# Block transposes from the tenth couple of heads on, with their loads, squares and sums moved

## The chip, the cores and the metric

The kernel runs on one core of a Trainium2 chip. Its engines work side by side, each through its own queue in order: TensorE (PE in the profile; its weight loads are PEld), VectorE (DVE), ScalarE (ACT), GpSimd (POOL) and SyncE (SP), which here issues nearly all DMAs. The metric is the device time of one execution in microseconds (us). All data is float32.

## The reference, cut to what matters

```python
q, k, v: (8, 12, 448, 64)      # batch, heads, sequence, head size
w_in: (768, 2048); w_out: (2048, 768)

def rmsnorm(x, g):
    return x / np.sqrt(np.mean(x * x, axis=-1, keepdims=True) + 1e-06) * g
scores = np.matmul(rmsnorm(q, g_q), rmsnorm(k, g_k).transpose(0, 1, 3, 2)) / np.sqrt(64)
attn = softmax(scores)                     # max subtracted, 1e-9 added to the sum
x = np.matmul(attn, v)                     # then (B,H,S,D) -> (B*S, H*D) = (3584, 768)
h = x @ w_in
out = (h * (1.0 / (1.0 + np.exp(-h)))) @ w_out
```

## The kernel before, in words

**Couples.** The 96 heads are handled in 24 couples of four heads (two pairs), three couples for each of the eight batches, six for each group of two batches (`GROUP` is 6). For couple c, `visit(c)` does the attention: 56 score matmuls (L726, each pair of records one matmul), exponentials on ScalarE (L731) that take k's norm as their scale, and 56 records of the weighted sum with v (L763). The softmax sums are made of the exponentials by adds on VectorE (`add`, L777) and a product with ones on TensorE (`sum_up`, L799). VectorE inverts them (L808), DMAs spread the factors over the partitions (L815, L817), and the next visit multiplies with them (L824).

**Hand-over.** After visit c comes `between(c)`, which prepares couple c+1 and fills TensorE with work of the feed-forward layer: products with `w_in` (L923) in the seven-product form of Strassen (class `Seven`), for the group of batches finished before. `fill` runs such matmuls up to a due amount, and deals other work between them: `others` evenly, one after so many steps, `prompt` one at the start and one after each product. There are two fills for a couple, called the first and the second half here. A step is one 448-column product of 128 rows (two records), three steps make a product. Products alternate between two PSUM banks (tile mm; `bank`); with `turns["third"]` and more than five steps due, every other product goes to a buffer of the scores' tile (sc) instead. A product is evicted by VectorE (L873) or by ScalarE (L931, L941), two additions of the seven go to GpSimd (L943, L944), and the finished rows get SiLU (L1061) and are stored to a scratch tensor `hidden` (L956).

**Two ways to transposed q and k.** q and k must lie with the head dimension on the partitions. Up to couple 11 TensorE transposes them: q with 8 matmuls (`transpose_q`, L643), k with 7 (`transpose_k`, L661). ScalarE copies both out of PSUM (L647, and L663, which multiplies with the gains). q's norm comes from squares on ScalarE (L470) and reductions on VectorE (L471), two for each half of q, then a power and a product on GpSimd (L499, L514). From couple `LATE` = 12 on q and k are loaded in quarters, so that VectorE's transpose of 32x32 blocks is enough (`load_quarters`, L253: eight DMAs of 128-byte runs; `flip`, L669 for q, L672 for k, then the gains on ScalarE, L678). q's squares are then taken in one operation (L686) and reduced in one (L687); TensorE adds the two halves of each head (`scale`, L698, with the identity changed once by `pair_up`), and GpSimd does power and product (L702, L705). k is loaded a second time by rows, for its norm (L285, L287, squares L470, L471). From couple 8 on q has only one place, q0; the places k0 and k1 serve couples in turn, and from `LATE` on k0 holds the rows and k1 the quarters.

**Other work in couples 6 to 11.** The last parts of `w_in` are loaded and rounded there: `weights_in` deals steps named r (`round`: three operations on VectorE, L124, L127, L131, then one on GpSimd, L135, then a load, L86) and o (`open`: two on ScalarE, L101 and L102) into the halves. Visits 8 and 10 hold two rounds each, and visits 7 and 9 four sums of weights each (`sum_w_in`, L870, L873). The remaining four sums stand in `sums_halves`: three in the first half of couple 10, one in its second.

**What sets the order.** It is written out by hand: the program order of each engine is the order of the calls. A queue that waits holds back all that was issued on it later. Couple numbers begin at 0, so couple 9 is the tenth.

Of the kernel before, what the change touches and what calls it, by code (L numbers as in the profile page):

```python
# [30 lines left out]
class Shapes:  # L31
    def __init__(self, q, w_in):
        self.B, self.H, self.S, self.D = q.shape
        self.DM, self.DFF = w_in.shape
        self.P = 128
        self.J = 4
        self.R = self.S // self.J
        self.NPAIR = self.H // 2
        self.NW = self.DM // self.P
        self.NF = self.DFF // self.P  # L40
        self.HALF = self.DM // 2
        self.FULL = self.S // self.P
        self.REST = self.S - self.FULL * self.P

        self.KEYS = self.S // self.P
        self.LEFT = self.S - self.KEYS * self.P
        assert 2 * self.LEFT == self.P and self.NPAIR % 2 == 0 and self.LEFT == self.D

        self.KA, self.KL, self.KB = 0, 2 * self.KEYS * self.D, 2 * (self.KEYS + 1) * self.D
        self.NK = self.KB + 2 * self.KEYS * self.D  # L50
        assert 2 * self.D == self.P and self.J * self.R == self.S and 2 * self.REST == self.P
        assert self.NW == self.NPAIR and self.B % 2 == 0

        self.LATE = 2 * self.NPAIR
        self.Q = 32
        assert 2 * self.S == self.NK and 4 * self.Q == self.P and self.D == 2 * self.Q

# [136 lines left out]
def kernel(  # L194
# [77 lines left out]

    def load_k_quarters(c):
        b, cp = divmod(c, z.NPAIR // 2)
        load_quarters(k[b, ts(cp, 4)], place["k1"])

    def load_k(c):
        t = place[f"k{c % 2}"]
        if c >= z.LATE:
            t = place["k0"]  # L280
            for i, start in enumerate((z.KA, z.KB)):
                main, left = plain(k, c, i)
                dst = t[:, ds(start, z.KL)].rearrange("p (j h d) -> p h j d", j=z.KEYS, h=2)
                for h in range(2):
                    nc.sync.dma_start(dst[:, h], main[:, h])  # L285
                dst = t[ds(i * z.LEFT, z.LEFT), ds(z.KL, 2 * D)]
                nc.sync.dma_start(dst.rearrange("p (h d) -> p h d", h=2), left)  # L287
            return
        main, left = keys_of(k, c)
        for i, start in enumerate((z.KA, z.KB)):  # L290
            dst = t[:, ds(start, z.KL)].rearrange("p (j h d) -> p j h d", j=z.KEYS, h=2)
            nc.sync.dma_start(dst, main[:, ts(i, 2)].rearrange("p h j d -> p j h d"))
            if i == 0:
                for m in range(2):
                    dst = t[ds(m * z.LEFT, z.LEFT), ds(z.KL, 2 * D)]
                    nc.sync.dma_start(dst.rearrange("p (h d) -> p h d", h=2), left[m])
# [242 lines left out]
def bounded(  # L539
# [12 lines left out]
    )  # L552
    GROUP, LATE = z.NPAIR, z.LATE
    EARLY = GROUP - 1


    hidden = dram.tile([z.NF, P, z.B * S], F32, name="hidden")
# [42 lines left out]
    def q_of(c):  # L600
        return rows_q[c % 2 if c < GROUP + 2 else 0]

    def load_q(c):

        if 0 < c < NC:
            loads["q"](c, raw_of(c) if c < GROUP else q_of(c))
# [59 lines left out]
    def flip(c, name):  # L666

        if name == "q":
            nc.vector.transpose(qT.rearrange("p i s -> p (i s)"), q_of(c)[:, 0 : z.NK])  # L669
            load_q(c + 1)  # L670
            return
        nc.vector.transpose(kT, place["k1"])  # L672
        if c + 1 < NC:
            loads["quarters"](c + 1)

# [3 lines left out]

    n = z.NK // z.Q  # L680

    def sum_squares(c):

        if c >= NC:
            return
        nc.scalar.activation(squares, q_of(c)[:, 0 : z.NK], AF.Square)  # L686
        nc.vector.tensor_reduce(  # L687
            out=norm.rms[c % 2][:, 0:n], in_=squares.rearrange("p (n e) -> p n e", e=z.Q),
            axis=AX.X, op=ALU.add,
        )  # L690
# [90 lines left out]
    def sum_up(c):  # L781

        n = D // 2
        early = c < GROUP
        t = bank(S) if c < GROUP else ps.tile([P, 2, BANK], F32, name="sc", bufs=2)[:, 0, 0:S]
        terms = [(0, lambda: weights(c, 0))]
        if early:  # L790
            terms = [(0, lambda: weights(c, LEFT - 1))] + terms + [(1, None)]
        if c == GROUP - 1:
            terms.insert(1, (0, lambda: weights(c, 1)))
        for k, (which, w) in enumerate(terms):
            if k == len(terms) - 2:
                yield
            for h in range(2):
                for i in range(2):
                    nc.tensor.matmul(  # L799
                        t[ds(h * D + i * n, n), :],  # L800
                        ones[:, which + i if which else 0],
                        left_weights(c)[:, h] if which else w()[:, i, h],
                        start=(k == 0), stop=(k == len(terms) - 1),
                    )

        def invert(half):
            rows = ts(half, S // 2)
            nc.vector.reciprocal(out=factors(c)[0][:, rows], in_=t[:, rows])  # L808

        def spread():  # L810
            mine = [a.rearrange("(h i p) s -> i h p s", h=2, i=2) for a in factors(c)]
            queues = (nc.sync, nc.gpsimd if c == GROUP - 1 else nc.sync)
            for h in range(2):
                for i in range(2):
                    queues[h].dma_start(mine[1][i, h], mine[0][1, h])  # L815
            for h in range(2):
                queues[h].dma_start(mine[0][1, h], mine[0][0, h])  # L817

        yield [lambda: invert(0), lambda: (invert(1), spread())]
# [8 lines left out]
    def normalise(c):  # L828


        def piece(name, i):
            t = scratch[i if c < GROUP + 2 else 0]
            source = raw_of(c) if c < GROUP else q_of(c)
            if name == "q":
                norm.squares_q(c, source, t, i)
            else:
                norm.squares_k(c, place["k0" if c >= LATE else f"k{c % 2}"], t, i)
            if name == "q" and c < GROUP:
                norm.root(c, name, i)
                norm.scale(c, source, q_of(c), i, nc.gpsimd)  # L840
                if i == 1 and c + 2 < GROUP:
                    load_q(c + 2)
            elif i == 1:
                norm.root(c, name)
                if name == "q":
                    for m in range(2):
                        norm.scale(c, source, q_of(c), m, nc.gpsimd)
                elif LATE <= c < NC - 1:
                    loads["k"](c + 1)

        if c >= NC:
            return []
        return [lambda a=a: piece(*a) for a in (("q", 0), ("q", 1), ("k", 0), ("k", 1))]
# [419 lines left out]
    def save_out(q, i, j):  # L1273
        for t in range(2):
            store(
                nc, out, z, (4 * q + 2 * (i - 1) + t) * P, results[i, j][t], (j - 1) * z.HALF,
                nc.gpsimd if q == QUADS - 1 and i == 2 else nc.sync, plain=4,
            )

    def quad(q):  # L1280
# [53 lines left out]
        if q == QUADS - 1:  # L1334

            def then(t, h):
                store(
                    nc, out, z, (4 * q + t) * P, c[1, 2][t][:, ts(h, QUARTER)],
                    z.HALF + h * QUARTER, *((nc.scalar, nc.sync)[:: 1 if h else -1]), plain=4,
                )  # L1340

            deep(3, c[1, 2], True, None, then)
            return
# [51 lines left out]
    for c in range(GROUP // 2):  # L1395
        halves[2 * (c - GROUP)], halves[2 * (c - GROUP) + 1] = "rr", "o"
    sums_halves = {-6: [(0, 0)], -4: [(0, 1)], -3: [(0, 2)], -2: [(0, 3)]}
    sums_halves[8] = [(3, step) for step in range(3)]
    sums_halves[9] = [(3, 3)]
    sums_visits = {GROUP + 1: 1, GROUP + 3: 2}  # L1400

    def weights_in(c, half):
# [90 lines left out]
    def between(c):  # L1493
# [30 lines left out]
        if c >= GROUP and c % GROUP == 0:  # L1524
# [2 lines left out]
            work = halves_in(last_two(c), range(HF), plain_in, dict(begun), fetched)  # L1527
            begin(work, columns, 2 * GROUP)
            begun.clear()
        late = add(c, LEFT - 1) + add(c, LEFT) if c >= GROUP else []  # L1530
        further = normalise(c + 2) if c >= GROUP - 1 else []
        fill(late + weights_in(c, 0) + (further[2:] if c >= GROUP else further[:2]))
        prompt = transposes_and_sums() if GROUP // 2 <= c != GROUP - 1 else []
        if prompt and c < GROUP:
            prompt.insert(0, lambda: None)
# [2 lines left out]
        if c >= LATE - 2:  # L1538
            if c == LATE - 2:
                prompt.append(pair_up)  # L1540
            queries = prompt[3:] + [lambda: sum_squares(c + 2)]
            steps = weights_in(c, 1)
            fill(steps + [lambda: None] * len(steps), prompt[:3] + [lambda: run_all(queries)])
        else:
            fill(weights_in(c, 1) + (further[:2] if c >= GROUP else []), prompt)
# [258 lines left out]
```

## Time and profile before

| | |
|---|---|
| runs | 1311.65, 1312.07, 1312.16 us; median 1312.07 |
| profiled execution | 1311.68 us, span 1309.9 us |
| mean granted TensorE clock | 0.999 |
| TensorE's transposes, q (L643, records of tile rows) | 60 records, 7.5 us busy |
| TensorE's transposes, k (L661) | 84 records, 11.6 us busy |
| ScalarE's copies out of PSUM (L647, L663) | 11 of 906 ns and 12 of 1002 ns |
| factors' product on TensorE (L698) | 24 records, 3.6 us busy |
| sums on TensorE in tile sc (L799) | 144 records, 18.5 us busy |

The span runs from the first to the last instruction, and the execution's time has a little more around it. Busy times of an engine that are hidden beside TensorE's cost nothing. A matmul's record ends after the next has begun, so TensorE's work is read from the distance between the starts of its records.

### The profile page before, as it was taken

To read this page: it belongs to the slowest core of one execution; us is meant where nothing else is said; L and a number is where in the kernel's file an instruction comes from. 1 tells how busy PE (TensorE), PEld (TensorE's weight loads), DVE (VectorE), ACT (ScalarE), POOL (GpSimd) and SP (SyncE) were. 2 spreads that over 40 slices of the span, in tenths; PEclk is the share of its full clock that TensorE was granted. 3 is DMA by queue.
4 is the path that set the end of the run, shared out by engine and by line. 5 is a ranking of instruction groups with operands and counts; after the bars stand their busy time and mean duration, and the time that the engine had idled before them with its cause. 6 is when DMAs were issued, how large, how long until landed. Compare 5 with 4: busy or idle time off the path is not lost.

```text
span 1309.9 us, 19866 instructions
## 1 busy us (share of the span) xinstructions
PE 1294.2 (99%) x7209; PEld 832.3 (64%) x7209; DVE 950.1 (73%) x1627; ACT 505.0 (39%) x886; POOL 360.8 (28%) x230
## 2 busy tenths in 40 slices
PE   9999999999999999999999999999999999999998
PEld 4444444444444444444444455558999999999998
DVE  6998777777655556755554786698978787878785
ACT  7866656645544545545544354310000000100000
POOL 6766544453334333334320244300000000000000
PEclk9999999999999999999999999999999999999999
DMA  9674335344443444444321457312323223231411
GB/s 242 169 198 121 100 98 164 113 95 110 108 94 90 121 96 95 98 113 95 83 68 63 141 191 253 125 61 78 106 81 101 85 95 110 68 127 52 136 42 40
DMA packets 249439, 144.94 MB, mean 111 GB/s; under 512 B 184292, under 2 KB 233220, under 8 KB 249332
## 3 DMA queue, kind: packets, MB, share of 16 engines
q1 hardware_dynamic: 248672, 142.42, 38.8%
q8 instruction: 59, 0.97, 0.3%
q0 software_dynamic: 352, 0.96, 0.2%
q14 instruction: 48, 0.39, 0.1%
q10 hardware_dynamic: 308, 0.20, 0.1%
HBM read 93.98 MB, written 41.29 MB: 103 GB/s over the span
## 4 chain that ended last, share of the span: by engine, by line
PE 94%; DVE 2%; ACT 2%; issue 1%; POOL 0%; ACTq 0%; DVEq 0%; POOLq 0%
PE alone L1230 23%; PE mm L923 22%; PE av L763 9%; PE sc L726 9%; PE sc L923 9%; PE mm L1230 8%; PE alone L923 7%; PE alone L1267 2%; PE sc L799 1%; PE mm L799 1%; PE mm L1267 1%; PE sc L643 1%; PE sc L661 1%; ACT work L731 1%; DVE work L777 0%
## 5 line engine op out<-in xcount | busy, mean ns | idle before, releaser
L731 ACT ACTIVATE work<-sc,rms 128x448 f32<-128x448 f32 x318 | 181.1, 634 | 63.1 <-PE sc L726 50.4
L923 PE MATMUL mm<-x,W 128*128 128x448 f32 x414 | 169.9, 545 | 4.0 <-DVE parts L873 1.8
L726 PE MATMUL sc<-work 64*64 64x448 f32 x1344 | 164.1, 544 | 1.8 <-ACT work L731 1.5
L777 DVE TENSOR_TENSOR work<-work 128x896 f32<-128x896 f32 (+1 forms) x114 | 124.6, 1125 | 50.0 <-PE av L763 49.5
L923 PE MATMUL mm<-sums_x,W 128*128 128x448 f32 x372 | 152.5, 543 | 0.5 <-DVE parts L873 0.5
L763 PE MATMUL av<-work,rows 64*64 64x448 f32 x1272 | 150.7, 540 | 0.5 <-DVE av L739 0.3
L499 POOL TENSOR_TENSOR rms<-rms,minus_half 128x14 f32<-128x14 f32 (+4 forms) x43 | 105.4, 2453 | 148.2 <-DVE rms L495 138.6
L923 PEld LDWEIGHTS mm<-x,W 128*128 128x128 f32 x414 | 76.4, 190 | 87.2 <-issue 73.7
L526 POOL DMA_DIRECT2D out_dram<-x x2 | 1.2, 592 | 443.3 <-DVE x L873 443.3
L923 PEld LDWEIGHTS mm<-sums_x,W 128*128 128x128 f32 x372 | 69.2, 190 | 73.7 <-issue 68.0
L1230 PE MATMUL alone<-W,rows 128*128 128x192 f32 x610 | 113.0, 326 | 0.0
L763 PEld LDWEIGHTS av<-work,rows 64*64 64x64 f32 x1272 | 57.8, 132 | 69.1 <-issue 33.8
L1230 PEld LDWEIGHTS alone<-W,rows 128*128 128x128 f32 x610 | 101.5, 190 | 0.0
L726 PEld LDWEIGHTS sc<-work 64*64 64x64 f32 x1344 | 52.9, 132 | 74.1 <-ACT work L731 30.8
L943 POOL TENSOR_TENSOR parts<-parts,stage 128x448 f32<-128x448 f32 x31 | 41.9, 1351 | 146.7 <-DVE parts L873 146.3
L923 PE MATMUL sc<-x,W 128*128 128x448 f32 x198 | 80.6, 543 | 0.0
L702 POOL TENSOR_TENSOR rms<-rms,minus_half 128x28 f32<-128x28 f32 x12 | 57.5, 4792 | 61.7 <-DVE rms L699 61.7
L1230 PE MATMUL alone<-W,work 128*128 128x192 f32 x382 | 72.2, 326 | 0.0
L1061 ACT ACTIVATE stage<-stage 128x896 f32<-128x896 f32 x63 | 57.3, 945 | 21.9 <-DVE stage L873 21.0
L1240 ACT COPY rows<-alone 128x192 f32<-128x192 f32 x33 | 10.5, 318 | 141.6 <-PE alone L1230 78.2
L1230 PEld LDWEIGHTS alone<-W,work 128*128 128x128 f32 x382 | 63.8, 190 | 0.0
L923 PEld LDWEIGHTS sc<-x,W 128*128 128x128 f32 x198 | 36.9, 190 | 39.6 <-issue 37.2
(259 smaller groups left out, 2283.6 us busy)
## 6 DMA issues: line engine op xcount, KB each, us to landing
hidden<-stage SPq DMA_DIRECT2D x63, 448.0 KB, 3.2
work<-hidden SPq DMA_DIRECT2D x21, 1024.0 KB, 5.1
rows<-in_moe_w_out_dram SPq DMA_DIRECT2D x32, 384.0 KB, 3.3
W<-in_moe_w_in_dram SPq DMA_DIRECT2D x22, 512.0 KB, 5.2
x<-hidden SPq DMA_DIRECT2D x7, 1024.0 KB, 6.4
work<-work SPq DMA_DIRECT2D x111, 56.0 KB, 2.0
rows<-in_q_dram SPq DMA_DIRECT2D x96, 56.0 KB, 2.2
rows<-in_k_dram SPq DMA_DIRECT2D x96, 56.0 KB, 2.2
```

What stands on the lines that cost most here:

```text
L499: nc.gpsimd.tensor_tensor(out=t, in0=t, in1=half, op=ALU.pow)
L702: nc.gpsimd.tensor_tensor(out=f, in0=f, in1=minus_half.to_broadcast([P, n]), op=ALU.pow)
L726: nc.tensor.matmul(two[ds(half * D, D), h, 0:S], keys[rows, ts(half, D)], qT[rows, pair, :], start=True, stop=True,)
L731: nc.scalar.activation(left_weights(c)[:, h] if j == LEFT else weights(c, j)[:, i, h], two[:, h, 0:S], AF.Exp, scale=norm.column(c, i, h, j),)
L763: nc.tensor.matmul(sums[i][ds(h * D, D), :], v, w, start=(j == 0 and step == 1), stop=(j == LEFT - 1 and step == 1),)
L777: nc.vector.tensor_tensor(out=total, in0=total, in1=more, op=ALU.add)
L799: nc.tensor.matmul(t[ds(h * D + i * n, n), :], ones[:, which + i if which else 0], left_weights(c)[:, h] if which else w()[:, i, h], start ...
L923: nc.tensor.matmul(t, self.left(name, s), self.right(name, s), start=s == ends[0], stop=s == ends[1])
L943: nc.gpsimd.tensor_tensor(out=u2, in0=u2, in1=p5, op=ALU.add)
L1061: nc.scalar.activation(t, t, AF.Silu)
L1230: nc.tensor.matmul(t, x[:, i], y, start=i == ORDER[0], stop=i == ORDER[-1])
L1267: nc.tensor.matmul(o, a[:, 2 * i + m, t], right_one(name, i)[:, m], start=n == 0, stop=n == len(steps) - 1,)
```

## The change

Couples 9, 10 and 11 are loaded in quarters too and transposed in blocks by VectorE. As couple 9 is odd, k0 and k1 change roles for the late couples. The result's rows are stored in plain order from batch 3 on.

For the hand-overs from couple 8 to couple 10, q's load for the couple after next is no longer issued in `flip` at the start of the half but in the middle of the first half's `others`. For the hand-overs from 7 to 10 the squares of q are dealt together with the third prompt piece (pair_up in 7, k's flip after), one product before their reduction. The third bank is closed for the second half in all hand-overs before 11. In couple 10 the left-over sums aren't added on VectorE any more: `sum_up` takes four matmuls more, straight from the left-over weights. Of the last four sums of weights two stand in each half of couple 10.

```diff
-        self.LATE = 2 * self.NPAIR
+        self.LATE = 3 * self.NPAIR // 2
+        self.PLAIN = 3
+        self.BY_ROWS, self.BY_QUARTERS = f"k{self.LATE % 2}", f"k{1 - self.LATE % 2}"
...
     def load_k_quarters(c):
         b, cp = divmod(c, z.NPAIR // 2)
-        load_quarters(k[b, ts(cp, 4)], place["k1"])
+        load_quarters(k[b, ts(cp, 4)], place[z.BY_QUARTERS])
...
         if c >= z.LATE:
-            t = place["k0"]
+            t = place[z.BY_ROWS]
...
+    SOON = 2 * GROUP - 1
+    FULL = SOON - 1
...
             nc.vector.transpose(qT.rearrange("p i s -> p (i s)"), q_of(c)[:, 0 : z.NK])
-            load_q(c + 1)
+            if c > SOON:
+                load_q(c + 1)
             return
-        nc.vector.transpose(kT, place["k1"])
+        nc.vector.transpose(kT, place[z.BY_QUARTERS])
...
+    def square(c):
+
+        if c < NC:
+            nc.scalar.activation(squares, q_of(c)[:, 0 : z.NK], AF.Square)
+
     def sum_squares(c):
 
         if c >= NC:
             return
-        nc.scalar.activation(squares, q_of(c)[:, 0 : z.NK], AF.Square)
...
         if early:
             terms = [(0, lambda: weights(c, LEFT - 1))] + terms + [(1, None)]
+        if c == FULL:
+            terms.insert(0, (1, None))
...
-            if k == len(terms) - 2:
+            if early and k == len(terms) - 2:
                 yield
...
-    sums_halves[8] = [(3, step) for step in range(3)]
-    sums_halves[9] = [(3, 3)]
+    sums_halves[8] = [(3, 0), (3, 1)]
+    sums_halves[9] = [(3, 2), (3, 3)]
...
-        late = add(c, LEFT - 1) + add(c, LEFT) if c >= GROUP else []
+        late = add(c, LEFT - 1) if c >= GROUP else []
+        if c >= GROUP and c != FULL:
+            late += add(c, LEFT)
         further = normalise(c + 2) if c >= GROUP - 1 else []
-        fill(late + weights_in(c, 0) + (further[2:] if c >= GROUP else further[:2]))
+        late += weights_in(c, 0) + (further[2:] if c >= GROUP else further[:2])
+        if LATE - 1 <= c < SOON:
+            late.insert(len(late) // 2, lambda: load_q(c + 2))
+        fill(late)
+        if c < SOON:
+            turns["third"] = False
...
             queries = prompt[3:] + [lambda: sum_squares(c + 2)]
+            turning = prompt[2:3] + [lambda: square(c + 2)]
+            if c < SOON:
+                prompt[2:3] = [lambda: run_all(turning)]
+            else:
+                queries.insert(len(queries) - 1, lambda: square(c + 2))
```

More of the change, by code (lines that the diff above doesn't have):

```diff
@@ L836, in piece @@
             else:
-                norm.squares_k(c, place["k0" if c >= LATE else f"k{c % 2}"], t, i)
+                norm.squares_k(c, place[z.BY_ROWS if c >= LATE else f"k{c % 2}"], t, i)
             if name == "q" and c < GROUP:
@@ L1276, in save_out @@
                 nc, out, z, (4 * q + 2 * (i - 1) + t) * P, results[i, j][t], (j - 1) * z.HALF,
-                nc.gpsimd if q == QUADS - 1 and i == 2 else nc.sync, plain=4,
+                nc.gpsimd if q == QUADS - 1 and i == 2 else nc.sync, plain=z.PLAIN,
             )
@@ L1338, in then @@
                     nc, out, z, (4 * q + t) * P, c[1, 2][t][:, ts(h, QUARTER)],
-                    z.HALF + h * QUARTER, *((nc.scalar, nc.sync)[:: 1 if h else -1]), plain=4,
+                    z.HALF + h * QUARTER, *((nc.scalar, nc.sync)[:: 1 if h else -1]), plain=z.PLAIN,
                 )
```

## The prediction

> **What bounds the kernel now.** I read, in this order: the busy shares, the chain that ended last, the stretches couple by couple (from the first score product of a couple to that of the next), the groups of the operations concerned, and the timeline where TensorE waited.
>
> ```profile
> PE 1294.2 (99%) x7209; PEld 832.3 (64%) x7209; DVE 950.1 (73%) x1627; ACT 505.0 (39%) x886; POOL 360.8 (28%) x230
> PE 94%; DVE 2%; ACT 2%; issue 1%; POOL 0%; ACTq 0%; DVEq 0%; POOLq 0%
> ...
> 230.54 9.79 PE mm L923 x26
> ...
> 150.45:184.66 34.21, 33.59 (x188) 16.35 (x188) 24.32 (x34) 19.91 (x34) 14.55 (x10) 1.00 0.46 134
> 184.66:218.56 33.90, 33.90 (x188) 16.16 (x188) 24.87 (x35) 21.14 (x35) 15.76 (x10) 1.00 0.43 126
> 218.56:251.88 33.32, 33.32 (x188) 16.40 (x188) 24.92 (x32) 21.24 (x36) 13.30 (x8) 1.00 0.43 126
> 251.88:287.68 35.80, 34.52 (x190) 15.50 (x189) 29.51 (x35) 19.97 (x32) 17.30 (x13) 1.00 0.42 110
> 287.68:319.64 31.96, 31.96 (x175) 15.21 (x174) 18.31 (x24) 15.56 (x25) 12.51 (x7) 1.00 0.35 85
> ```
>
> TensorE carries 94% of the chain, so the end is moved by TensorE's work and by its waits. 26 fill records take 9.79 us, 0.376 us each; a product is six records, 2.26 us. The stretches are couples 7 to 11. All have the same fill (69,888 columns over 12 halves: 52 records a couple). Couple 11 already hands over by block transposes and takes 31.96 us; couple 9, with TensorE's transposes and no stall, takes 33.32. So the route is worth 33.32 - 31.96 = 1.36 us a couple where nothing waits. Couple 8 has 0.58 us and couple 10 2.15 us more than that (35.80 - 33.32 - 0.33 for the factors' product of couple 12, which it has already).
>
> ```profile
> L669 DVE STREAM_TRANSPOSE work<-rows 128x896 f32<-128x896 f32 x12 | 13.3, 1105 | 0.0
> L687 DVE TENSOR_REDUCE rms<-rows 128x28 f32<-128x896 f32 x12 | 13.0, 1085 | 16.7 <-ACT rows L686 16.7
> L702 POOL TENSOR_TENSOR rms<-rms,minus_half 128x28 f32<-128x28 f32 x12 | 57.5, 4792 | 61.7 <-DVE rms L699 61.7
> ...
> 190.92 0.43 DVE L127 TENSOR_SCALAR W<-W 128x512 int32<-128x512 int32 x1
> 192.44 1.40 DVE L127 TENSOR_SCALAR W<-W 128x512 int32<-128x512 int32 x1
> ...
> 211.19 0.30 PEld L923 LDWEIGHTS mm<-sums_x,W 128*128 128x128 f32 x2 [0.63 <-DVE parts L873]
> ...
> 212.99 0.62 DVE L873 TENSOR_TENSOR stage<-mm,parts 128x448 f32<-128x448 f32 x1 [0.39 <-POOL parts L943]
> ...
> 213.67 0.30 PEld L923 LDWEIGHTS mm<-x,W 128*128 128x128 f32 x2 [0.68 <-DVE stage L873]
> ...
> 216.11 0.30 PEld L923 LDWEIGHTS mm<-x,W 128*128 128x128 f32 x2 [0.64 <-DVE stage L873]
> ...
> 253.12 0.63 ACT L470 ACTIVATE rows<-rows 112x512 f32<-112x512 f32 x1 [0.75 <-DVE rms L471]
> 256.37 0.61 PE L726 MATMUL sc<-work 64*64 64x448 f32 x4 [0.50 <-ACT work L731]
> 285.62 0.53 ACT L941 COPY stage<-mm 128x448 f32<-128x448 f32 x1 [3.46 <-DMA hidden<-stage]
> 286.60 1.02 PE L923 MATMUL mm<-x,W 128*128 128x448 f32 x2 [0.72 <-DVE parts L873]
> ```
>
> The first three rows price the new route; the two L127 rows are one operation without and with GpSimd at work. At 211.19 to 216.11 (couple 8, second half) each weight load waits for an eviction by VectorE: products alternate between two PSUM banks, so product n+2 starts when product n is evicted, and VectorE has no slack there. At 253.12 and 256.37 (hand-over 9 to 10) ScalarE is still at squares when scores come. At 285.62 ScalarE waits for a store that SyncE issued only after 16 quarter loads and 6 row loads.
>
> **What the Trainium skill says.** "Perfetto Trace Analysis", section Identifying the Most-Contended Engine: matmul busy share is a poor measure. Agrees: couple 8 shows 33.90 of 33.90 busy and has waits; I go by the spacing of matmuls. "SBUF — State Buffer", section Who interferes with whom: a VectorE operation in a two-port mode or with two SBUF inputs blocks with GpSimd; one with one input outside those modes, and a reduction, doesn't. L127's 0.43 against 1.40 us agrees; that the block transpose is free of it no run here shows. "VectorE: DVE Perf Modes", section The three transpose paths: VectorE transposes 32x32 blocks only, so q and k must come in quarters; the trace gives 1.105 us for 128x896. "DMA: Bandwidth & Descriptors", section Specifications: full rate from 512 B; quarters are runs of 128 B. Still, the eight of couple 12 each land some 2.5 us after issue; it is SyncE's 0.52 us per issue that counts.
>
> **The change part by part** (hand-overs 8 to 9, 9 to 10, 10 to 11; the one from 7 to 8 prepares them).
>
> *Hand-over 7.* TensorE still transposes; added is couple 9's factors' product (in couple 10 0.23 us, from 287.46 to the scores at 287.69, and some 0.1 for the switch of tile shape before it: 0.33, on the path). SyncE has 8+6+8+6 issues in place of 2+4+6: from the k squares at 173.0, rows to 176.3, quarters to 180.6, the reciprocals' spread to 185, landed by 187, against its use by the division at 189.3: covered by 2 us. No store is due in between. The copies of pair_up (four, 0.26 us apart in couple 10) come on GpSimd before L943, which an eviction waits for; the next half's first product needs that bank. Between 0 and 1 us; I take 0.5. The old wait of 0.8 us at 176 stays. Sum: couple 7 +0.8 (+0.3 to +1.3).
>
> *Couple 8.* Gone: TensorE's 15 transposes, ScalarE's copy of 0.9 us. In place, on VectorE: q's flip (1.1) at the start of half one, k's flip (1.1) and the reduction (1.1) in half two; the two q reductions that go (0.69 and 0.68) stand behind the evictions today and free nothing. Walk along VectorE with couple 8 starting 0.8 late: GpSimd's power and product for couple 9 (4.8 + 1.8) end near 192.2; the rounding in the visit is blocked by them about 1 us longer than now, so the adds end at 199.2, flip 200.3, two adds, one left-over add, eviction, second left-over add 204.9, eviction 205.4, rounding 207.0, k's squares and reductions 209.0. Today that point is 209.1: the wait of 2.31 us that VectorE has there absorbs it (its cause, ScalarE's wait for a store behind q's loads, goes as q's loads move behind the stores). First reciprocal, eviction 210.9: product 7 waits to 210.95 (0.65 us late), second reciprocal, L943 behind GpSimd's power to 212.8, eviction 213.4 (0.3 late), k's flip 214.4, rounding 215.9, eviction 216.5 (0.75 late). 31.96 + 1.7 = 33.7 against 33.90: only 0.2 gained. Bounds: 31.96 (no wait) to 35.1 (the flip too is blocked by L944, and the first-half chain 1 us later).
>
> *Couple 9.* Four sums of weights stand in the visit; the adds end near 230.9, flip 232.0. In half one a third bank is open, so late evictions cost nothing; the product that needs the second reciprocal's predecessor starts 0.35 late. Half two: rounding and flip fit before the eviction that product 9 needs. 31.96 + 0.35 = 32.3 against 33.32: 1.0 gained (bounds 0 and 1.36). ScalarE's squares are a product sooner, so its first exponential of visit 10 comes about 1 us after the scores, not 2.8; couples 13 on have 1.5 there and no stall.
>
> *Couple 10.* The left-over sums on TensorE: four matmuls more in sum_up, two records of 0.376 in depth, +0.75. VectorE loses two adds (1.1 and 1.9 us today) and gets two flips; the four weight sums are spread two and two. My walk has the first-half chain end at 274.2, as TensorE's sums end at 274.3, and every later eviction 0.5 to 0.7 us before its bank is needed. Stores go out before quarters, so the wait at 285.62 goes, and that of 256.37. 31.96 + 0.75 + 0.2 (rounding in the visit) = 32.9 against 35.80: 2.9 gained (bounds 1.4, if the store still comes late, and 3.1).
>
> *After.* Couples 11 on run the same code without stall; the stores of batch 3 in plain rows lie beside TensorE's work at the end. Nothing there takes a gain back.
>
> Sum: -0.8 + 0.2 + 1.0 + 2.9 = 3.3 us off the profiled execution's 1311.68 (span 1309.9 and 1.8 around it). The median of the runs is 0.4 above that execution: 1312.07 - 3.3 = 1308.8.
>
> **The rivals.**
> *B, TensorE-bound throughout.* VectorE catches up inside the couples and only 0.33 is paid at hand-over 7: -0.33 + 1.94 + 1.36 + 3.09 = 6.1, time 1306.0. For: couples 11 and 13 to 17 run so. Against: these have no rounding and no sums, couple 8 has both at once.
> *C, taken back.* Couple 8 loses 0.5, couple 9 gains nothing and couple 10's late store stays (1.4): with 0.8 paid, 0.1 us; a little better gives 1 us, 1311. For: VectorE bounds couple 8 today, so TensorE's transposes were partly hidden. That the shorter TensorE work is not on the path at all, the change not doing what it says, is this case too.
> *D, slower: VectorE's queue becomes the bound in all three couples.* Place: evictions behind flip, rounding and reciprocals. Price per couple: flips 2.2, reduction 1.1, GpSimd's block 1.7, less q's reductions and their small step 1.5: 3.5 against 1.36 saved, 2.1 lost; three times 6.4, with 0.8 at hand-over 7, less couple 10's stalls of 2.2: +5.0, time 1317. It decides once an eviction comes over one product (2.26 us) after its product's end. For: couple 8. Against: VectorE is busy 24.9 of 33.3 us in couple 9, and a third bank is open in half one.
>
> **How the numbers follow.** A (as worked out) 0.52, its own range 1307.2 to 1310.4; B 0.17; C 0.20; D 0.11. About 0.2% (2.6 us) is what can be told from no change, so faster is below 1309.4: most of A (0.44) and B, 0.61; within: the rest of A and nearly all of C, 0.27; slower: D and a tail of C, 0.12. The likeliest is A's 1308.8. Range 1305.6 to 1313.4: B's end below, C's above, with D left out.
>
> **What would show it.** Right: L643 and L661 gone from couples 9 to 11; stretches of about 35.0, 33.7, 32.3, 32.9 and again 31.96; couple 8's second half with TensorE behind VectorE's evictions; no wait of ScalarE for a store near 285. Wrong: couple 8 at 32 (B), couples 9 or 10 with product starts behind VectorE (D), waits on the spread in the division of visit 8, or a new wait at hand-over 7 over 1 us.

## The result, and the profile after

| | before | after |
|---|---|---|
| median of 13 runs each | 1312.07 us | 1309.43 us (1308.60 to 1311.17) |
| ratio, 95% interval | | 0.9981 [0.9973, 0.9989] |
| profiled execution, span | 1311.68, 1309.9 us | 1311.17, 1309.4 us |

The change gains 2.6 us, 0.2%; the repeats of both kernels below give 2.3. The profiled execution of after happens to be the slowest of its 13: couple 4 took 22.17 us in it, against 20.55 in a repeat and 20.57 before, and it ran before anything the change touches. So the reading goes by couples, not by the whole span. Line numbers are up to 11 higher than before (L923 is now L934, L873 L884, L941 L952, L956 L967, L808 L819, L731 L740, L669 and L672 L673 and L677). These are the stretches of couples 7 to 11 in after, from the first score product to the next couple's; the columns are the stretch, the busy time of TensorE, its weight loads, VectorE, ScalarE and GpSimd with instruction counts, the granted clock, the DMA share and GB/s.

```profile
152.18:187.03 34.85, 33.97 (x190) 16.80 (x189) 24.76 (x33) 20.88 (x34) 15.35 (x14) 1.00 0.54 143
187.03:221.61 34.58, 32.96 (x175) 14.90 (x174) 26.97 (x35) 20.45 (x32) 17.47 (x9) 1.00 0.49 125
221.61:254.12 32.51, 32.27 (x175) 15.02 (x174) 27.99 (x35) 20.22 (x35) 14.84 (x7) 1.00 0.58 142
254.12:286.88 32.76, 32.76 (x183) 15.49 (x182) 26.22 (x32) 18.26 (x29) 15.49 (x7) 1.00 0.50 126
286.88:318.84 31.96, 31.96 (x175) 15.21 (x174) 18.30 (x24) 15.57 (x25) 13.50 (x7) 1.00 0.42 96
```

| couple | before | predicted | after | after, repeat |
|---|---|---|---|---|
| 7 | 34.21 | 35.0 | 34.85 | 34.86 |
| 8 | 33.90 | 33.7 | 34.58 | 35.26 |
| 9 | 33.32 | 32.3 | 32.51 | 32.52 |
| 10 | 35.80 | 32.9 | 32.76 | 32.76 |
| 11 | 31.96 | 31.96 | 31.96 | 31.96 |
| sum | 169.19 | 165.9 | 166.66 | 167.36 |

What is to be seen: the gain comes from couple 10 (3.0) and couple 9 (0.8), couple 7 pays 0.6, and couple 8, where 0.2 was to be gained, loses 0.7 to 1.4. Couple 11 and those behind it give nothing back. Two rows of the costliest groups show the new route itself at its old price, with 15 couples in place of 12:

```profile
L673 DVE STREAM_TRANSPOSE work<-rows 128x896 f32<-128x896 f32 x15 | 16.5, 1103 | 0.0
L677 DVE STREAM_TRANSPOSE work<-rows 128x896 f32<-128x896 f32 x15 | 16.1, 1075 | 0.0
```

Couple 10 had two waits before: scores waited for ScalarE at 256.37, at its start, and ScalarE waited 3.46 us for a store at 285.62, near its end. The first row is from the timeline of before, the others from that of after (start, duration, engine, line, and in brackets the idle time before it):

```profile
282.87 0.89 SPq L956 DMA_DIRECT2D hidden<-stage  x2
...
255.50 1.14 ACT L740 ACTIVATE work<-sc,rms 128x448 f32<-128x448 f32 x2
...
280.37 0.34 SPq L967 DMA_DIRECT2D hidden<-stage  x1
...
283.90 0.53 ACT L952 COPY stage<-mm 128x448 f32<-128x448 f32 x1
```

The store now leaves SyncE at 280.37 (282.87 before), L952 has no wait, and visit 10's first exponential starts 1.4 us after its first score product (254.12), where before it was 3.3 us (255.17 and 251.88).

Couple 8 is where the forecast missed. Its first half before, by engine (SPq is SyncE's queue, whose times are of issuing):

```profile
197.14 0.43 SPq L329 DMA_DIRECT2D rows<-in_v_dram  x1
197.61 1.34 SPq L332 DMA_DIRECT2D rows<-in_v_dram  x2
199.00 0.59 SPq L316 DMA_DIRECT2D rows<-in_v_dram  x1
199.70 2.14 SPq L266 DMA_DIRECT2D rows<-in_q_dram  x2
201.93 1.10 SPq L956 DMA_DIRECT2D hidden<-stage  x2
...
206.07 0.53 ACT L941 COPY stage<-mm 128x448 f32<-128x448 f32 x1 [3.12 <-DMA hidden<-stage]
...
209.11 1.55 DVE L808 RECIPROCAL work<-sc 128x224 f32<-128x224 f32 x1
```

And after, with the two late products of the second half at the end:

```profile
196.69 3.52 SPq L88 DMA_DIRECT2D W<-in_moe_w_in_dram  x2
200.26 0.43 SPq L325 DMA_DIRECT2D rows<-in_v_dram  x1
...
202.82 2.70 SPq L314 DMA_DIRECT2D rows<-in_v_dram  x4
205.62 0.89 SPq L967 DMA_DIRECT2D hidden<-stage  x2
206.60 5.09 SPq L255 DMA_DIRECT2D rows<-in_q_dram  x8
...
206.45 0.62 DVE L884 TENSOR_TENSOR parts<-mm,stage 128x448 f32<-128x448 f32 x1
...
207.13 1.77 PE L934 MATMUL mm<-x,W 128*128 128x448 f32 x4 [0.59 <-DVE parts L884]
...
208.37 0.53 ACT L952 COPY stage<-mm 128x448 f32<-128x448 f32 x1 [3.78 <-DMA hidden<-stage]
...
209.47 0.69 DVE L473 TENSOR_REDUCE rms<-rows 128x8 f32<-128x512 f32 x1 [0.87 <-ACT rows L472]
...
211.41 1.55 DVE L819 RECIPROCAL work<-sc 128x224 f32<-128x224 f32 x1
...
213.50 2.52 PE L934 MATMUL mm<-sums_x,W 128*128 128x448 f32 x6 [0.50 <-DVE parts L884]
...
219.03 2.52 PE L934 MATMUL mm<-x,W 128*128 128x448 f32 x6 [0.53 <-DVE stage L884]
```

Two things are to be seen. q's eight loads are behind the stores, as intended. But in front of the stores stand eight loads of v (L325, L327, L314, from 200.26 to 205.5); before the change four stood there, from 197.14 to 199.6, and two of q behind them. v's loads also begin later, 13.2 us into the couple in place of 12.5. So the stores leave 18.6 us after the couple's start (205.62 - 187.03), in place of 17.3 (201.93 - 184.66). ScalarE's eviction L952 needs the stage buffer that the store empties, k's squares wait behind it, and VectorE's reductions, reciprocals and evictions behind those. The second: at 207.13 TensorE starts a product 0.75 us late, in the first half already, because its bank was evicted at 206.45 to 207.07.

### The profile page after: what moved, and what is told of

It is laid out like the page before. It is cut to its first block, busy times and chain, and to the rows that moved or that the text cites. A ratio compares the mean times of both kernels' runs of the same rounds, so it can differ in the third digit from the quotient of the medians.

```text
span 1309.4 us, 19898 instructions
## 1 busy us (share of the span) xinstructions
PE 1291.4 (99%) x7178; PEld 828.3 (63%) x7178; DVE 951.8 (73%) x1628; ACT 502.7 (38%) x880; POOL 363.9 (28%) x227
## 4 chain that ended last, share of the span: by engine, by line
PE 78%; DVE 2%; ACT 1%; issue 1%; DMA 0%; SPq 0%; ACTq 0%; DVEq 0%
PE alone L1241 23%; PE mm L934 16%; PE sc L934 9%; PE mm L1241 8%; PE alone L934 7%; PE av L772 6%; PE sc L735 6%; PE alone L1278 2%; PE sc L810 1%; PE mm L1278 1%; ACT work L740 0%; DVE work L884 0%; DVE work L786 0%; DVE stage L884 0%; ACT L1579 0%
## 5 line engine op out<-in xcount | busy, mean ns | idle before, releaser
L740 ACT ACTIVATE work<-sc,rms 128x448 f32<-128x448 f32 x318 | 181.3, 634 | 72.9 <-PE sc L735 57.1
L934 PE MATMUL mm<-x,W 128*128 128x448 f32 x396 | 163.4, 546 | 4.7 <-DVE stage L884 1.7
L934 PE MATMUL mm<-sums_x,W 128*128 128x448 f32 x360 | 147.6, 543 | 1.0 <-DVE parts L884 1.0
L501 POOL TENSOR_TENSOR rms<-rms,minus_half 128x14 f32<-128x14 f32 (+4 forms) x40 | 95.7, 2394 | 135.1 <-DVE rms L497 131.1
L934 PEld LDWEIGHTS mm<-x,W 128*128 128x128 f32 x396 | 72.9, 190 | 85.8 <-issue 70.8
L934 PEld LDWEIGHTS mm<-sums_x,W 128*128 128x128 f32 x360 | 67.0, 190 | 72.8 <-issue 67.0
L711 POOL TENSOR_TENSOR rms<-rms,minus_half 128x28 f32<-128x28 f32 x15 | 71.9, 4794 | 67.3 <-DVE rms L708 60.9
L934 PE MATMUL sc<-x,W 128*128 128x448 f32 x216 | 87.9, 543 | 0.0
L934 PEld LDWEIGHTS sc<-x,W 128*128 128x128 f32 x216 | 40.4, 190 | 42.9 <-issue 40.6
```

Source lines behind the costliest of these rows:

```text
L501: nc.gpsimd.tensor_tensor(out=t, in0=t, in1=half, op=ALU.pow)
L711: nc.gpsimd.tensor_tensor(out=f, in0=f, in1=minus_half.to_broadcast([P, n]), op=ALU.pow)
L740: nc.scalar.activation(left_weights(c)[:, h] if j == LEFT else weights(c, j)[:, i, h], two[:, h, 0:S], AF.Exp, scale=norm.column(c, i, h, j),)
L934: nc.tensor.matmul(t, self.left(name, s), self.right(name, s), start=s == ends[0], stop=s == ends[1])
```

## The experiments

All are edits of the kernel after. "Stretch" is from a couple's first score product to the next one's, in the profiled execution. Couple 8 takes 34.58 in one profile of the kernel after and 35.26 in another, while the other four couples repeat within 0.02; so for couple 8 only differences above 0.7 us are read.

**Repeats of both kernels.**

> The changed kernel once more, to see how far its stretches repeat. In the first four runs couples 9, 10 and 11 came within 0.05 us of each other, and couple 8 differed by up to 1 us where the edit shouldn't reach. Theory (couple 8 hangs on when a store lands, and that differs from run to run): couple 8 anywhere from 34.5 to 35.3, couple 7 34.85, couples 9 to 11 as before. Rival (couple 8 is fixed at 34.6, and the edits made it longer): 34.6 within 0.05.

Measured: 1309.41 us, ratio 0.9983 [0.9975, 0.9991]; its stretches stand in the table above. Before, repeated: 1311.76 us, stretches 34.21, 33.97, 33.33, 35.83, 31.96.

**Pair_up one product later in hand-over 7.**

```diff
-            if c == LATE - 2:
-                prompt.append(pair_up)
             queries = prompt[3:] + [lambda: sum_squares(c + 2)]
+            if c == LATE - 2:
+                queries.insert(0, pair_up)
```

> pair_up's four copies go one product later, behind GpSimd's two additions. Theory (the copies hold up L954, and with it the eviction that couple 7's last product waits for): the wait of 0.42 us near the end of couple 7 goes, its stretch falls from 34.85 to about 34.4, the rest as in the changed kernel. Rival (that product waits for VectorE's rounding and reductions anyway): couple 7 stays at 34.8 to 34.9. In the time: at most 0.4 us.

Measured: 1309.20 us, 0.9978 [0.9970, 0.9987]; couple 7 34.41, couple 8 35.19. The wait that follows GpSimd's copies in hand-over 7 is 0.42 us in after (distance 0.797 between two records) and gone here: that is the price of pair_up's place. Couple 8 stays within its scatter: no gain from starting sooner is to be seen.

**Couple 8's left-over sums on TensorE too**, as in couple 10. This sets the lack of time on VectorE against the late store.

```diff
-        if c == FULL:
+        if c in (FULL - 2, FULL):
             terms.insert(0, (1, None))
...
-        if c >= GROUP and c != FULL:
+        if c >= GROUP and c not in (FULL - 2, FULL):
             late += add(c, LEFT)
```

> Couple 8's left-over sums go to TensorE too, as couple 10's do: two adds (1.0 and 1.1 us) off VectorE's first half, 0.75 us more on TensorE. Theory (ScalarE's wait for a late store sets VectorE's first reciprocal, and all evictions of the second half hang on it): only the first half's wait of 0.75 us goes and is paid for by TensorE's 0.75; couple 8 stays at 34.6 within 0.3. Rival (the amount of VectorE's work in couple 8 is the bound): the reciprocals come 1 to 2 us sooner and couple 8 falls to 33.3 or below.

Measured: 1310.43 us, 0.9990 [0.9983, 0.9996]; couple 8 35.63. It was expected at 34.6 within 0.3, which was set against a single profile of after; from the repeat it is 0.4 off. The wait of the first half is gone, but the next one, for the first reciprocal's eviction, grew from 0.67 (1.36 in the repeat) to 1.8 us. Its timeline:

```profile
207.42 0.53 ACT L952 COPY stage<-mm 128x448 f32<-128x448 f32 x1 [4.80 <-DMA hidden<-stage]
...
208.51 0.69 DVE L473 TENSOR_REDUCE rms<-rows 128x8 f32<-128x512 f32 x1 [4.04 <-ACT rows L472]
```

Without the two adds VectorE is through with its rounding 2.1 us sooner (19.5 us into the couple, 21.6 in after), and it stands idle for that and more: 4.04 us before the reduction, where it was 0.87. What sets the reciprocal is the store.

**Couple 8's first-half stores issued by ScalarE**, to free them from SyncE's queue.

```diff
+    saving = [nc.sync]
...
-        nc.sync.dma_start(hidden[f, :, ds(column, t.shape[1])], t)
+        saving[0].dma_start(hidden[f, :, ds(column, t.shape[1])], t)
...
-        fill(late)
+        saving[0] = nc.scalar if c == LATE - 1 else nc.sync
+        fill(late)
+        saving[0] = nc.sync
```

> Only the two stores of couple 8's first half are issued by ScalarE, straight after its SiLU, instead of by SyncE behind eight loads of v. Theory (late store, then L952, then k's squares, then the first reciprocal): ScalarE's wait of 3.8 us for the store goes, the first reciprocal comes 0.9 us sooner, and the second half's waits fall from 1.5 to about 0.6; couple 8 from 34.6 to 33.7. Rival (VectorE's amount of work): no earlier reciprocal, 34.6; the two issues on ScalarE cost up to 1 us there.

Measured: 1310.06 us, 0.9987 [0.9981, 0.9994]; couple 8 35.45. The experiment didn't do what it was for:

```profile
203.60 0.37 ACTq L969 DMA_DIRECT2D hidden<-stage  x1
204.03 0.95 ACT L1074 ACTIVATE stage<-stage 128x896 f32<-128x896 f32 x1 [3.51 <-DMA rows<-in_v_dram]
```

ScalarE's issue was itself held, by the profile until a load of v had landed, and with it the SiLU behind it. It tells nothing on the store theory. Why that issue waits for a load of v the trace doesn't show.

**q's loads back at the start of the half.**

```diff
-            if c > SOON:
-                load_q(c + 1)
+            load_q(c + 1)
...
-        if LATE - 1 <= c < SOON:
-            late.insert(len(late) // 2, lambda: load_q(c + 2))
```

> q's loads go back into the flip at the start of the half, ahead of the stores. Theory (SyncE's order decides when the store lands): in couple 8 the stores go out some 4 us later, k's squares and the first reciprocal 3 to 4 us later, and TensorE waits for it: couple 8 about 37.5 to 38.5; couple 10 is hit less, since its stores come in the second half, couple 9 not at all. In all 3 to 4 us slower than the changed kernel, that is slower than the kernel before by about 1. Rival (the place of q's loads doesn't matter as long as they land in time): all stretches as in the changed kernel.

Measured: 1314.18 us, 1.0018 [1.0009, 1.0027], slower than before the change; couple 8 38.84, the others unchanged, couple 10 too, where a small loss was expected. SyncE's queue and ScalarE in couple 8 (L951 and L966 are L952 and L967 of after):

```profile
203.92 4.07 SPq L255 DMA_DIRECT2D rows<-in_q_dram  x8
208.08 0.90 SPq L966 DMA_DIRECT2D hidden<-stage  x2
...
210.88 0.53 ACT L951 COPY stage<-mm 128x448 f32<-128x448 f32 x1 [8.05 <-DMA hidden<-stage]
```

Eight issues more ahead of the store, and ScalarE waits 8.05 us. Without this move the whole change would have been a loss. In couples 9 and 10 the place of these loads is indifferent.

**The loads of v for couple 9 moved out of visit 8 to where q's are** (with pair_up later as above). This tests the store theory by its own cause.

```diff
-            if c + 1 < NC:
+            if c + 1 < NC and c != LATE - 1:
                 loads["vrest"](c + 1)
...
-        if c + 1 < NC:
+        if c + 1 < NC and c != LATE - 1:
             loads["v"](c + 1)
...
-            late.insert(len(late) // 2, lambda: load_q(c + 2))
+            at = len(late) // 2
+            late.insert(at, lambda: load_q(c + 2))
+            if c == LATE - 1:
+                late[at:at] = [lambda: (loads["vrest"](c + 1), loads["v"](c + 1))]
```

> pair_up one product later as in e1_pair_later; besides, couple 9's eight loads of v leave visit 8 and stand with q's loads in the middle of the first half, so that the stores have SyncE free when SiLU is done. Theory (late store, then L952, then k's squares, then the first reciprocal): the store is issued about 3 us sooner, ScalarE's wait before L952 shrinks from about 4 us to the wait for TensorE, the first reciprocal comes 1.0 to 1.5 us sooner, and couple 8 falls to 33.6 to 34.2; couple 7 34.4. Some 1.2 us less than the changed kernel in all, 1308.2. Rival (VectorE's amount of work is the bound): couple 8 stays at 34.6 to 35.3.

Measured: 1307.64 us, 0.9967 [0.9955, 0.9979]; couples 7 to 11 34.41, 33.60, 32.52, 32.76, 31.96. Its timeline in couple 8:

```profile
200.58 1.44 SPq L967 DMA_DIRECT2D hidden<-stage  x2
202.06 0.46 SPq L325 DMA_DIRECT2D rows<-in_v_dram  x1
...
204.57 0.53 ACT L952 COPY stage<-mm 128x448 f32<-128x448 f32 x1 [2.03 <-PE mm L934]
...
208.39 1.55 DVE L819 RECIPROCAL work<-sc 128x224 f32<-128x224 f32 x1
```

The store goes first, L952 waits for its product alone, the first reciprocal comes 23.4 us into the couple in place of 24.4 to 25.1, and couple 8 takes 33.60 us, where the prediction had worked out 33.7. That eight loads of v ahead of the stores made couple 8 late is shown. VectorE doesn't wait before its reduction any more: its own work now sets the reciprocal, as the next run shows.

**The same with couple 8's left-over sums on TensorE.**

> e8_v_late and besides couple 8's left-over sums on TensorE as in e2_left8. With the store out of the way VectorE's amount of work should now set the reciprocals: the wait of 0.75 us in the first half goes, which pays for TensorE's 0.75, and the reciprocals come up to 1 us sooner. Theory: couple 8 at 33.0 to 33.7, 0.3 to 1 us below e8_v_late. Rival (something else holds the reciprocals): no better than e8_v_late, or worse by the 0.75.

Measured: 1307.13 us, 0.9967 [0.9955, 0.9979]; the stretch of couple 8:

```profile
184.82:217.67 32.85, 32.85 (x183) 15.40 (x182) 24.97 (x33) 19.75 (x32) 17.33 (x9) 1.00 0.49 127
```

The edit that cost 1.0 us with a late store (1310.43 against 1309.41) now takes 0.75 us off the couple: no record in it waits for an eviction. The times of the two kernels can't be told apart by their runs (1307.64 and 1307.13, six each), the stretches can. Couples 7 to 11 sum to 164.48, against 166.66 and 167.36 in after; five of its six runs lie below the fastest of after's first 13.

**k's remaining squares ahead of the weights' copies in couple 7**, on top of that, against the wait of 0.79 us that before and after both have, 26.5 us into the couple.

```diff
-        late += weights_in(c, 0) + (further[2:] if c >= GROUP else further[:2])
+        parts_of = [weights_in(c, 0), further[2:] if c >= GROUP else further[:2]]
+        late += sum(parts_of[:: -1 if c == LATE - 2 else 1], [])
```

> Pair_up one product later, the v loads moved into the first half, couple 8's left-over sums on TensorE, and one thing more: in couple 7's first half k's remaining squares are taken on ScalarE ahead of the copy of weights and the SiLU that delay them. Theory: the wait of 0.79 us before couple 7's sixth product is for an eviction that sits behind a reciprocal that sits behind these squares, so couple 7 goes from 34.4 to about 33.6 us, couples 8 to 11 stay at 32.85, 32.5, 32.8 and 31.96 us, and the time is about 1306.4 us. Rival: the wait only changes its reason (VectorE's own queue is as late, or the copy that is now later delays the output of the couple before), couple 7 stays within 0.2 of 34.4 and the time at 1307.1 us.

Measured: 1307.98 us, 0.9970 [0.9958, 0.9981]; couple 7 35.37, 1.0 longer. Theory and rival both missed: the old wait stays at 0.79, as the rival had it, but one of 0.75 comes before it. VectorE in the timeline:

```profile
171.94 0.69 DVE L473 TENSOR_REDUCE rms<-rows 128x8 f32<-128x512 f32 x1 [3.35 <-ACT rows L472]
...
173.88 0.62 DVE L884 TENSOR_TENSOR stage<-mm,stage 128x448 f32<-128x448 f32 x1
...
175.94 1.55 DVE L819 RECIPROCAL work<-sc 128x224 f32<-128x224 f32 x1
```

The squares are followed on VectorE by their reductions, which now stand ahead of a rounding and an eviction. ScalarE is in a SiLU until 171.29, so VectorE waits 3.35 us, the eviction that ran at 170.09 runs at 173.88, and the reciprocal comes at 175.94 instead of 174.95.

**The third bank left open in the second halves.**

```diff
-        if c < SOON:
-            turns["third"] = False
```

> The changed kernel with the third bank left open in the second half too. Theory (in couple 8's second half product 7 waits for an eviction only because it has the bank of product 5): with the scores' buffer in turn product 7 starts at once, product 8 waits for the second reciprocal instead (that buffer holds the sums), and couple 8 falls from 35.26 to about 33.6 to 34.3; couple 9 loses its wait of 0.4; couple 10, which has none, may gain one of up to 1 us behind the reciprocals. Rival (products in the scores' buffer meet the sums and the factors' product there, and cost more than they save): couples 8 to 10 together longer than in the changed kernel.

Measured: 1308.11 us, 0.9973 [0.9964, 0.9983]; couple 8 33.57, couple 10 32.76 as before. The late store is still there (L952 waits 4.03 us for it), but the products of the second half have a third bank to go to. With the third bank closed couple 8 costs 1.0 to 1.7 us more. In couple 9 the wait of 0.40, which was expected to go, stays, but comes before another product (30.6 us into the couple instead of 26.1). Before the change hand-overs 8 to 10 had two banks in both halves: `LATE` now opens the third for the first half, and the new line shuts it for the second. That line is a part of the change that loses: without it the time is 1308.1, 1.3 less than after.

**q's square just ahead of its reduction again.**

```diff
-            turning = prompt[2:3] + [lambda: square(c + 2)]
-            if c < SOON:
-                prompt[2:3] = [lambda: run_all(turning)]
-            else:
-                queries.insert(len(queries) - 1, lambda: square(c + 2))
+            queries.insert(len(queries) - 1, lambda: square(c + 2))
```

> q's squares go back to just before their reduction, behind the gains on ScalarE. Theory (VectorE's order sets the pace, and the reduction comes after the last eviction in any case): couples 8 and 10 within 0.3 of the changed kernel, at most a late factors' product at the end of couple 7 or 8, 0.3. Rival (ScalarE's queue is as tight as VectorE's, and the squares a product sooner are what keeps the scores on time): 0.5 to 1 us longer in each of the three.

Measured: 1311.57 us, 0.9997 [0.9988, 1.0006]: 2.1 us more than after, nearly the whole gain. Couple 9 34.00, 1.5 more, of which the theory said nothing, and where the rival had 0.5 to 1; 7, 8 and 10 as in after. The other 0.6 us doesn't show in these couples. Its timeline at the end of couple 9:

```profile
252.40 0.93 ACT L690 ACTIVATE rows<-rows 128x896 f32<-128x896 f32 x1
...
253.37 1.09 DVE L696 TENSOR_REDUCE rms<-rows 128x28 f32<-128x896 f32 x1 [1.98 <-ACT rows L690]
...
254.51 0.41 PE L707 MATMUL sc<-rms,ident 128*128 128x28 f32 x2 [1.24 <-DVE rms L696]
```

ScalarE gets to the square 31.6 us into the couple, after two copies of weights and the gains of k (29.5 in after, ahead of them), and the factors' product, the last of the hand-over, waits for it.

**Couple 10's left-over sums back on VectorE.**

```diff
-        if c == FULL:
-            terms.insert(0, (1, None))
...
-        if c >= GROUP and c != FULL:
+        if c >= GROUP:
             late += add(c, LEFT)
```

> Couple 10's left-over sums go back to VectorE (two adds of 1.1 us more there, 0.75 less on TensorE). Theory of the prediction (every eviction of couple 10 comes 0.5 to 0.7 us before its bank is needed): TensorE wins 0.75 and then waits for evictions that are 2 us later, 1.3 to 1.5 in all; couple 10 at 33.3 to 33.6 in place of 32.77. Rival (couple 10 has slack enough, and TensorE's four matmuls are simply lost): 32.0. Other couples unchanged.

Measured: 1311.16 us, 0.9995 [0.9986, 1.0003]; couple 10 34.54, 0.9 above the most that was expected. From its timeline:

```profile
269.83 3.01 DVE L786 TENSOR_TENSOR work<-work 64x896 f32<-64x896 f32 x2
...
281.40 1.77 PE L932 MATMUL mm<-sums_x,W 128*128 128x448 f32 x4 [1.20 <-DVE stage L882]
```

The two adds take 3.01 us of VectorE in the first half, and TensorE then waits 0.9 and 1.4 us beyond the usual distance of 0.376. So four matmuls that cost TensorE 0.75 us save 1.8 net: more than half of what couple 10 gained.

## Why the prediction was right, and where it was off

The direction was right, and the mechanism is the one foreseen: TensorE's transposes gone and couple 10's stalls gone with them. 3.3 us were worked out, 2.6 measured by the medians (2.3 in the repeat); the five couples of the profiles gain 2.5 (1.9 in the repeat), and nearly all that is missing is couple 8's.

*Hand-over 7, +0.8.* Measured +0.64. pair_up's copies cost 0.42 where 0.5 was taken (shown by moving them); the division of visit 8 waits for no spread.

*Couple 9, 32.3.* Measured 32.51. The 0.35 for a product behind a reciprocal is 0.40. What the prediction mentioned only for ScalarE's first exponential, the earlier square, carries it: without it the couple takes 34.00, longer than before the change. That its cost would fall on the factors' product was not foreseen.

*Couple 10, 32.9.* Measured 32.76. Both old waits are gone and no record waits for an eviction: 31.96, 0.75 for the sums and 0.05 of visit.

*Couple 8, 33.7: the term that was mis-sized.* The step that failed is "ScalarE's wait for a store behind q's loads, goes as q's loads move behind the stores". q's loads did move, but v of couple 9 changes its layout with them (`load_v` and `load_v_rest` ask for `LATE` too), which neither the description of the change nor the prediction mentions, and its four issues became eight in the same place ahead of the stores. The wait went from 3.12 to 3.78 us (4.47 in the repeat) instead of going.

What that costs can be read from one date, the start of couple 8's first reciprocal. All times are us from the couple's first score product:

| profile | ScalarE's eviction L952 | first reciprocal | end of couple 8 |
|---|---|---|---|
| before (L941, L808) | 21.41 | 24.45 | 33.90 |
| predicted | | 23.54 | 33.7 |
| after | 21.34 | 24.38 | 34.58 |
| after, repeat | 22.03 | 25.07 | 35.26 |
| couple 8's sums on TensorE | 22.40 | 25.44 | 35.63 |
| q's loads early | 25.60 | 28.65 | 38.84 |
| v's loads moved | 19.58 | 23.40 | 33.60 |

Where L952 waits for a store, the reciprocal follows it by 3.0 us. From the reciprocal to the end of the couple it is 10.2 us in all nine profiles of the new order with two banks in the second half, whatever TensorE does in between: the second reciprocal, k's flip, the rounding and the last evictions follow one another. (Before, it was 9.45: after is longer by this work, not by a later reciprocal. With the third bank open it is 8.9, and with the sums on TensorE and v's loads moved TensorE has no wait left.) The prediction had this right: 23.54 (209.0 - 185.46, the start that it walked from) and 10.2 make 33.7. Its walk along VectorE was also right within 0.1 us from the flip (14.84 against 14.76) to the end of the rounding (21.54 against 21.56). So the whole miss is the 0.84 us by which the reciprocal came later than walked, 1.53 in the repeat: the store was counted on to come sooner and didn't. With v's loads moved the reciprocal comes at 23.40.

One wait was overlooked that has no price of its own. The eviction of the first half ended where the walk had it, 20.0 us into the couple, but the product that needs its bank was due 0.75 us before. With v's loads moved this wait is still there, and the couple takes 33.60: a product that is late here is so much less late behind the reciprocal. The waits were worked out as 0.65, 0.3 and 0.75, all in the second half; with v's loads moved they are 0.74 in the first half and 0.69 at the last product. With 0.1 us behind each, as below, that is 1.6 against 1.7: the sum was right, not the places. (In after they are 0.75, 0.67, 0.12 and 0.69. The record that follows each wait comes 0.48 us after the late one instead of 0.376, and 31.96 + 0.75 + 1.48 + 0.4 = 34.6.)

*The rivals.* C (taken back) describes couple 8 alone, which lost 0.7 to 1.4 where C said 0.5. B (TensorE bound throughout, 1306.0) comes about in couple 8 in the version with v's loads moved and the sums on TensorE, whose time of 1307.1 us lies between A's and B's. D, VectorE as the bound in all three couples, didn't come: in after VectorE's evictions set the end of couple 8 alone, couple 9 has one product 0.40 us late and couple 10 none, and no product waits as long as another takes. The runs show how near it was: with q's loads left in place, or with the adds or the square left in theirs, the time is at 1311 to 1314 us.

The fastest version found is after with pair_up one product later, couple 9's v loaded in the first half and couple 8's left-over sums on TensorE. The third bank left open besides was not run. What is left in couple 7, the wait of 0.79 us, is open: the one attempt on it made it worse.

## What to carry to other kernels

When a data layout changes, list every tensor that takes it and count the DMA issues of each on the queue that also issues the stores: a move that clears the queue of one tensor can be filled up by another. When walking along an engine, walk along the queue that frees its buffers too: here the dates of VectorE were right within 0.1 us up to the one that hung on a store. To find what sets a stretch, look for an event from which its end keeps the same distance in all profiles. Taking work off an engine shows only once the wait that idles it is gone, so an edit without effect is worth trying again after the other cause is removed.

## What the hardware showed that was not expected

*TensorE at half pace after a wait.* Where q's loads stayed early, TensorE stood idle 2.49 us (3.03 between records), and the next four distances between records were 0.91, 0.75, 0.75 and 0.75 us in place of 0.376. The stretches around it in that run:

```profile
208.40:211.40 3.00, 0.57 (x2) 0.00 (x0) 0.00 (x0) 0.52 (x2) 0.00 (x0) 0.99 0.98 321
211.40:216.00 4.60, 4.13 (x6) 1.77 (x6) 3.40 (x6) 3.01 (x6) 1.91 (x1) 0.64 0.75 214
```

The granted clock is 0.64 of full in the second. The four distances add 1.6 us, but cost couple 8 nothing that can be seen: its end is 10.2 us behind the first reciprocal as in the other profiles, and TensorE waits again for its last products (0.57 and 0.69 us). That it took more than the 38.5 expected is the reciprocal's doing, 4.3 us later than in after (3.6 than in its repeat). The Trainium skill, "TensorE: Matmul & The Clock Gate", section What's actually happening, has the clock fall to half after an idle window of about 3.4 us; here 2.5 us were enough, while 1.65 us idle (the run with couple 8's sums on TensorE alone) left the next records at 0.376.

*Block transposes beside GpSimd.* The prediction left open whether they are blocked. In couple 9 of after one has GpSimd's L137 beside it for 0.9 of its 1.10 us and takes no longer than q's, which have no GpSimd beside them (1104 ns against 1097 to 1106). k's without it are mostly shorter, 1051 to 1054 ns in eight of nine, so 0.05 us may be its doing, against 1.0 for a real block (L127, 1.40 in place of 0.43). This agrees with the Trainium skill, "SBUF — State Buffer", section Who interferes with whom, for one input outside the two-port modes. That bound of the range could have been left out.

*Scatter in one couple.* In four profiles whose code for couple 8 is the same (after, its repeat, pair_up later, the sums of couple 10 on VectorE) L952 comes 21.34, 22.03, 21.95 and 21.76 us into the couple, and the couple takes 34.58, 35.26, 35.19 and 35.00. The differences are the same: the whole scatter is the store's, which leaves SyncE 18.6 us into the couple in after and 19.0 in its repeat and lands 0.3 us later still there, while couples 9 to 11 repeat within 0.05 us where their code is unchanged.
